# Cluster codes turned in packs of four, two or one tile, two lower halves on GpSimd, and a newly planned order, in a routed attention and MLP kernel

## The chip, the cores and the metric

The kernel runs on one core of a Trainium2 chip. The core has TensorE (PE in the profile; its weight loads are the row PEld), VectorE (DVE), ScalarE (ACT), GpSimd (POOL) and SyncE (SP, which here only issues DMAs), each with its own queue of instructions that it works off in order. The metric is the device time of one execution in microseconds. It was 307.97 us before the change, the median of three runs (307.48 to 308.44).

## The reference

```python
# q, k, v: (4, 8, 768, 64), centroids: (8, 16, 64), w_in: (512, 2048), w_out: (2048, 512)
q_assign = argmax(einsum('bhsd,hcd->bhsc', q_n, c_n))      # q_n, k_n, c_n: divided by their norms
k_assign = argmax(einsum('bhsd,hcd->bhsc', k_n, c_n))
mask = q_assign[:, :, :, None] == k_assign[:, :, None, :]
scores = where(mask, q @ k.T / 8, -1e9)
attn = exp(scores - max) / (sum + 1e-9)
x = (attn @ v).transpose(0, 2, 1, 3).reshape(3072, 512)
h = x @ w_in
out = (h / (1 + exp(-h))) @ w_out
```

A query sees only those keys whose nearest of 16 centroids, by angle, is its own. The kernel does it with a code of 16 numbers per query and key that is 16384 (or a number like it) at the nearest centroid and 0 elsewhere: with the codes as 16 more rows under the 64 of q and k, one matmul of 80 rows gives score and mask together, and the exponential makes the unmasked ones vanish.

## The kernel before

Work comes in four batches of eight heads; a head has six tiles of 128 queries and keys, and heads go in four pairs. Every pair goes through these stages:

- **Loads.** SP loads k, q and v of a pair as natural tiles nk, nq, nv (`load_k`, `load_q`, `load_v`; L374, L389, L404). v is cast to vt (L415, L417).
- **Part** (`part`, from L474). Each element of q and k is split in a high f16 half (L527 on ScalarE, L529 on VectorE, L531 on GpSimd) and a lower half, the rest (L535, VectorE), in a tile hl. The tiles are turned so that the 64 dimensions become partitions, multiplied with the centroids (logits), the best centroid is marked, and the marks are turned too, which gives the code rows.
 - In batches 1 to 3 a DMA turns the tiles (L550, `ab<-hl`); logits are L624, their sums L641, the peak L661, the distance L673 (GpSimd), the marks L700 and L702, and a 32x32 turn on VectorE (L715) gives ohT, from which four copies, one for each 32 columns, place the codes in ab (L732 on GpSimd three times, L728 as a DMA once; `PUTB` names the engines).
 - In batch 0 TensorE turns them: twelve or sixteen tiles of 128x128 (L570), a settle of eight at a time from PSUM to a tile lt (L585, L587), logits L615 and L619, peak L665, marks L690 (written beside the halves in hl, whose rows are 144 wide), and then a second turn of every tile, of its high half and its 16 marks, 80 rows (L570 again), and a settle with a gain for the code rows into ab (L581, L583).
- **Attention** (`attention`). Scores L801 fill a bank of 512 columns, one exponential on ScalarE (L808) makes P of it, PV is L829, and VectorE divides by the sum (L842, L847) into xn. A turn, on TensorE (L877, copies L882, L884) or by DMA (L866), gives xt. Batch 0 goes in two rounds, query tiles 0-1 of all heads and then 2-5, so that the MLP can start early.
- **MLP** (`mlp`). Nine units: batch 0 in three of two tiles, the others in two of three tiles. The 16 up matmul groups (L907), tanh (L913), the gate (L918) into gq, the down matmuls (L942), eviction into ot (L955 ScalarE, L957 VectorE; `EVAC` names one per unit), and the store (L960). `weight` loads the weights on the GpSimd queue (L976, L980), each released by an event of the program that `PW` names.

The order is written by a planner. Every operation is a `step` with an engine, a cost, what it follows, which buffers it holds and a key. `Plan.order` (a list schedule) takes again and again the step that can start first by its costs, the smaller key first among equals, gives it a buffer from a pool and appends it; the instructions are issued in that order, so the costs decide the order on every engine, but not the time. The keys come from `AT` and `ML` (due times of attention rounds and MLP units), `LEADS`, `REST`, `RLOAD` and `SOON` (how far ahead parts and loads go); the pools' sizes stand in `sizes`. Of TensorE's planned waits in the first 80 us (`UNREAD`) the planner fills those that it can with matmuls on zeros (L353), which nobody reads.

Of the kernel before, what the change touches and what calls it, by code (L numbers as in the profile page):

```python
# [11 lines left out]
f16 = mybir.dt.float16  # L12
AF = mybir.ActivationFunctionType
# [20 lines left out]
class Plan:  # L34
# [6 lines left out]
    EARLY = 700  # L41
    TURNED = 1000
    PORT = 0.75

# [4 lines left out]
    def step(self, eng, w, fn, after=(), use=(), key=0.0, load=None, hold=0.0, pace=None, flip=False, lag=None, slack=0.0, port=False):  # L49
# [4 lines left out]
        s.port = port or eng == "POOL"  # L54
# [20 lines left out]
    def order(self):  # L75
# [17 lines left out]
        def complete(s, end):  # L93
# [6 lines left out]
            for x in waits.get(s.n, ()):  # L100
                need[x.n] -= 1
                if not need[x.n]:
                    at = x.hold
                    for a in x.after:
                        late = a.end
                        if a.eng == x.eng and a.load is None:
                            late = a.start + a.w
                        at = max(at, late)
                    engines[x.eng]["ready"].append((at, x))

        def landing(until):

            while True:
# [6 lines left out]
                end = now + first[1] * len(active)  # L120
# [4 lines left out]
                for h in active:  # L125
                    h[1] -= (stop - now) / len(active)
                clock[0] = stop
                if stop == end:
                    s = first[2]
                    rings[s.eng].pop(0)  # L130
                    tail = self.TURNED if s.flip else self.EARLY if s.start < 2000 else self.LAND
# [67 lines left out]
def kernel(  # L199
# [28 lines left out]
    OHV = 16384.0  # L228
    VW = 72
    WN = 32  # L230
    HW = 2 * D + HC
# [6 lines left out]
    def many(name, n, shape, dt):  # L238
# [5 lines left out]
    stk = const.tile([128, H, 3 * HC], f16, name="stk")  # L244
    gain = const.tile([128, 1], f32, name="gain")
# [6 lines left out]
    chl = const.tile([128, 2, D], f16, name="chl")  # L252

    sizes = {
        "nk": (4, [128, 2, NJ * D], f32),
        "nq": (5, [128, 2, NJ * D], f32),
        "nv": (2, [128, 2, NJ * D], f32),
        "hl": (3, [128, 2 * (NJ + NA) * HW], f16),
        "lt": (2, [128, 2 * (NJ + NA), 128], f16),
        "ab": (5, [128, 24, 128], f16),  # L260
        "vt": (10, [128, NJ * VW], f16),
        "P": (18, [128, 512], f16),
        "gq": (7, [128, 4, MOST], f16),
        "xt": (3, [128, NR, S], f16),
        "xn": (3, [128, NJ, 128], f16),
        "L": (2, [128, 2 * NJ, HC], f32),
        "mx": (2, [128, 18], f32),
        "Df": (2, [128, 2 * NJ, HC], f32),
        "oh": (2, [128, 2 * NJ, 32], f16),
        "ohT": (3, [128, 2 * NJ, 32], f16),  # L270
        "tn": (3, [128, MOST], f32),
        "ot": (2, [128, DM], f32),
        "rz": (3, [128, NJ], f32),
    }
    T = {n: many(n, c, shape, dt) for n, (c, shape, dt) in sizes.items()}
    pools = {n: Pool(c) for n, (c, _, _) in sizes.items()}
# [23 lines left out]
    PW = [11, 5, 7, 13, 12, 27, 17, 2, 21, 10, 14, 19]  # L300
    UNREAD = 80000.0
    COLD = 8500.0
    MORE = 250.0
# [4 lines left out]
    VC = ["ACT", "ACT", "POOL", "ACT"]  # L308
    VB = "POOL"
    TK = ["ACT", "ACT", "DVE", "DVE", "DVE"]  # L310
    TQ = ["DVE", "ACT", "DVE", "DVE", "DVE"]
    TR = ["ACT", "DVE", "DVE", "DVE"]
    TS = ["ACT", "DVE", "DVE", "DVE"]
    HI = ["ACT", "ACT", "ACT", "POOL"]
    HR = ["DVE", "POOL", "DVE", "POOL"]
    LEADS = [27.5, 133.1, 88.1]
    REST = [3, 6, 3, 11]
    RLOAD = [2, 0, 3, 0]
    SOON = [7, 4, 7, 4]
    XT = ["DVE", "ACT", "ACT", "DVE"]  # L320
    EVAC = ["DVE", "DVE", "DVE", "DVE", "DVE", "DVE", "DVE", "ACT", "ACT", "DVE"]
# [4 lines left out]
    def consts_v():  # L326
        for t in T["oh"]:
            nc.vector.memset(t, 0.0)
        nc.vector.memset(stk, 0.0)
# [4 lines left out]
    def consts_p():  # L334
        nc.gpsimd.memset(half, 0.5)
        nc.gpsimd.memset(gain[0:64], 1.0)
        nc.gpsimd.memset(gain[64 : 64 + HC], OHV)
# [10 lines left out]
    s_ones = [v_ones(i) for i in range(sizes["vt"][0])]  # L348
# [17 lines left out]
    def load_k(b, p, key, eng="SP", hs=(0, 1), pace=None):  # L366
# [9 lines left out]
        s = step(eng, ISSUE, f, use=[x], key=key, load=657 * len(hs), pace=pace, slack=LATE if b else 0)  # L376
# [4 lines left out]
    def load_q(b, p, key, j0=0, j1=NJ, eng="SP", hs=(0, 1), pace=None):  # L381
# [9 lines left out]
        s = step(eng, ISSUE, f, use=[x], key=key, load=110 * (j1 - j0) * len(hs), pace=pace, slack=LATE if b else 300 if eng == "ACT" else 0)  # L391
# [7 lines left out]
    def load_v(b, p, key, pace=None):  # L399
# [6 lines left out]
        s = step("SP", ISSUE, f, use=[x], key=key, load=1310, pace=pace, slack=LATE if b else 0)  # L406
# [28 lines left out]
    def c_split():  # L435
        nc.vector.tensor_scalar(out=cz, in0=cy, scalar1=1e-6, scalar2=2.0 ** -11, op0=ALU.add, op1=ALU.mult)
        nc.vector.reciprocal(ci, cz)
        nc.vector.tensor_scalar(out=chl[:, 0, :], in0=craw, scalar1=ci, scalar2=None, op0=ALU.mult)
        nc.vector.scalar_tensor_tensor(
            out=chl[:, 1, :], in0=craw, scalar=ci, in1=chl[:, 0, :], op0=ALU.mult, op1=ALU.subtract  # L440
        )
# [3 lines left out]
    def c_turn():  # L445
        nc.tensor.transpose(banks[pc.i].bitcast(f16)[:, 0:128], chl.rearrange("p a d -> p (a d)"), ident)

    def c_place():
        pt = banks[pc.i].bitcast(f16)
        hi = pt[0:64, 0:128].rearrange("d (h c) -> d h c", c=HC)  # L450
        nc.vector.tensor_copy(stk[0:64, :, 0:HC], hi)
        nc.vector.tensor_copy(stk[64:128, :, 0:HC], hi)
        lo = pt[64:128, 0:128].rearrange("d (h c) -> d h c", c=HC)
        nc.vector.tensor_copy(stk[64:128, :, 2 * HC : 3 * HC], lo)

    def c_place_far():
        lo = banks[pc.i].bitcast(f16)[64:128, 0:128].rearrange("d (h c) -> d h c", c=HC)
        nc.vector.tensor_copy(stk[0:64, :, HC : 2 * HC], lo)

    s = step("ACT", 420, load_c, key=-100, load=60, slack=450)  # L460
    s = step("DVE", 400, c_sq, after=[s], key=-50)
    s = step("POOL", 500, c_root, after=[s], key=-90)
    s_split = s = step("DVE", 900, c_split, after=[s], key=-50)
    s = step("PE", 150, c_turn, after=[s, s_ident], use=[pc], key=-50)
    s_cent = step("DVE", 600, c_place, after=[s, s_const], use=[pc], key=-50)
    s_far = step("DVE", 200, c_place_far, after=[s, s_const], use=[pc], key=0)


# [5 lines left out]
    def part(b, p, segs, a0, due, lead=20.0, hi_eng="POOL", turn="DMA", twin=False, sub="POOL", code_eng=None, pace=None, wait=None):  # L474
# [10 lines left out]

        pitch, HI_AT = (2 * D, 0) if turn == "DMA" else (HW, D)

        def tiles_of(hl):
            return T["hl"][hl.i][:, 0 : n * pitch].rearrange("p (n c) -> p n c", c=pitch)

        t0 = 0
        runs = []
        for kind, h, j0, j1 in segs:
            runs.append((kind, h, j0, j1, t0))
            t0 += j1 - j0
        merged = []
        for r in runs:
# [595 lines left out]
```

## Time and profile before

| | |
|---|---|
| median of three runs | 307.97 us |
| profiled execution | 307.14 us, span of the instructions 305.3 us |
| busy: PE, DVE, ACT, POOL | 297.3, 207.9, 223.7, 108.2 us |
| first scores, first tanh, first batch logits | 11.8, 36.0, 51.6 us |
| DMA | 41.82 MB, mean 137 GB/s |
| granted TensorE clock | 0.998 |

The span is the time from the first to the last instruction of the program; the profiled execution's own time is 1.8 us longer. A group in the profile is one line of the kernel on one engine with what it writes and reads, its count, its busy time in us and the mean ns of one; behind the second bar stands how long the engine was idle before them and what ended that. In the chain and in timelines the first two numbers are start and length in us. A busy TensorE is not TensorE at its peak, since matmuls overlap; their distance from start to start says more.

### The profile page before, as it was taken

The page shows a single profiled execution, that of the slowest core. Times are in us where ns is not written, and L with a number is a line of the kernel's source. Part 1 is how long each engine was busy: PE and PEld are TensorE (multiplying, and loading weights), DVE is VectorE, ACT ScalarE, POOL GpSimd, SP SyncE. Part 2 cuts the span into 40 slices and gives each one's busy share as a digit, 9 for nine tenths or more (in the row PEclk, how much of TensorE's full clock was granted, in tenths as well). Part 3 has the DMA queues.
Part 4 walks back from the last instruction along what each step waited for, and adds up shares of the span by engine and source line. Part 5 has one row for each costly group of instructions (what it writes and reads, how often), then busy time and mean ns, then how long its engine had stood idle before and what let it go on. Part 6 is the DMA issues. An engine that isn't in the chain of part 4 may idle for free.

```text
span 305.3 us, 8425 instructions
## 1 busy us (share of the span) xinstructions
PE 297.3 (97%) x3257; PEld 196.1 (64%) x3257; DVE 207.9 (68%) x493; ACT 223.7 (73%) x461; POOL 108.2 (35%) x218
## 2 busy tenths in 40 slices
PE   8999999999999999999999998999999999999995
PEld 6898777577677746666656765665655565554644
DVE  5999688778869955989766997867562323750820
ACT  5869999888988838999777998778782380642721
POOL 2546432656466480717564563733000000000000
PEclk9999999999999999999999999999999999999999
DMA  7999969993969888486969848472010201002001
GB/s 245 290 249 251 206 104 224 103 248 87 226 100 237 191 167 196 138 156 162 237 149 223 155 154 169 131 129 66 0 37 36 84 12 71 35 0 73 32 34 69
DMA packets 73688, 41.82 MB, mean 137 GB/s; under 512 B 53041, under 2 KB 70705, under 8 KB 73649
## 3 DMA queue, kind: packets, MB, share of 16 engines
q1 hardware_dynamic: 68944, 36.94, 51.4%
q0 software_dynamic: 4288, 4.20, 8.6%
q8 instruction: 25, 0.41, 0.6%
q10 hardware_dynamic: 416, 0.16, 0.2%
q14 instruction: 15, 0.11, 0.1%
HBM read 27.30 MB, written 6.29 MB: 110 GB/s over the span
## 4 chain that ended last, share of the span: by engine, by line
PE 80%; DMA 7%; ACT 5%; DVE 3%; issue 1%; POOL 1%; SPq 0%; ACTq 0%; POOLq 0%
PE bank L942 27%; PE bank L907 22%; PE bank L801 16%; PE bank L829 9%; ACT P L808 4%; DMA ab<-hl 3%; PE bank L570 3%; DMA wout_s<-in_moe_w_out_dram 2%; PE bank L624 2%; DMA nk<-in_k_dram 2%; POOL hl L531 1%; PE bank L615 1%; DVE hl L535 1%; DVE gq L918 1%; PE bank L619 1%
## 5 line engine op out<-in xcount | busy, mean ns | idle before, releaser
L808 ACT ACTIVATE P<-bank 128x512 f16<-128x512 f32 x288 | 157.8, 640 | 30.8 <-PE bank L801 29.1
L942 PE MATMUL bank<-wout_s,gq 128*128 128x512 f16 (+1 forms) x400 | 97.1, 370 | 0.4 <-DMA wout_s<-in_moe_w_out_dram 0.4
L907 PE MATMUL bank<-xt,win_s 128*128 128x384 f16 (+1 forms) x576 | 95.6, 308 | 0.0
L918 DVE SCALAR_TENSOR_TENSOR gq<-tn,bank 128x384 f16<-128x384 f32 (+1 forms) x144 | 70.1, 504 | 32.4 <-ACT tn L913 28.7
L801 PE MATMUL bank<-ab 80*128 80x256 f16 (+1 forms) x384 | 90.9, 326 | 0.0
L913 ACT ACTIVATE tn<-bank 128x384 f32<-128x384 f32 (+1 forms) x144 | 67.8, 488 | 24.1 <-PE bank L907 20.9
L907 PEld LDWEIGHTS <-win_s 128*128 128x128 f16 x576 | 55.0, 97 | 28.8
L942 PEld LDWEIGHTS <-gq 128*128 128x128 f16 x400 | 37.9, 98 | 33.1 <-issue 0.7
L829 PEld LDWEIGHTS <-P 128*128 128x128 f16 x1152 | 45.6, 97 | 11.9 <-ACT P L808 0.8
L829 PE MATMUL bank<-vt,P 128*128 128x65 f16 x1152 | 49.8, 193 | 0.7 <-ACT P L808 0.6
L732 POOL COPY ab<-ohT 16x384 f16<-16x384 f16 x72 | 39.3, 546 | 28.2 <-DVE ohT L715 11.7
L801 PEld LDWEIGHTS <-ab 80*128 80x128 f16 x384 | 34.6, 97 | 20.7 <-DVE ab L583 0.2
L673 POOL TENSOR_TENSOR Df<-L,mx 128x192 f32<-128x192 f32 x24 | 12.3, 511 | 41.9 <-DVE mx L661 39.7
L957 DVE COPY ot<-bank 128x512 f32<-128x512 f32 x18 | 12.3, 681 | 16.4 <-PE bank L942 15.6
L535 DVE SCALAR_TENSOR_TENSOR hl<-nk,hl 128x384 f16<-128x384 f32 (+1 forms) x29 | 19.8, 687 | 3.3 <-POOL hl L531 3.1
L535 DVE SCALAR_TENSOR_TENSOR hl<-nq,hl 128x384 f16<-128x384 f32 (+3 forms) x33 | 20.9, 635 | 0.6 <-POOL hl L531 0.3
L641 DVE TENSOR_REDUCE L<-bank 128x192 f32<-128x384 f32 x24 | 13.3, 552 | 10.0 <-PE bank L624 9.7
L847 DVE TENSOR_TENSOR xn<-bank,rz 128x384 f16<-128x384 f32 (+2 forms) x40 | 19.1, 477 | 1.4 <-DVE rz L842 0.2
L531 POOL TENSOR_SCALAR hl<-nk 128x384 f16<-128x384 f32 (+1 forms) x25 | 13.6, 547 | 7.6 <-PE bank L570 6.7
L955 ACT COPY ot<-bank 128x512 f32<-128x512 f32 (+1 forms) x7 | 3.7, 524 | 17.2 <-PE bank L942 17.2
L531 POOL TENSOR_SCALAR hl<-nq 128x384 f16<-128x384 f32 (+2 forms) x27 | 15.2, 566 | 1.7 <-DMA nq<-in_q_dram 1.1
L417 POOL CAST vt<-nv 128x384 f16<-128x384 f32 x26 | 14.6, 582 | 1.1 <-DMA nv<-in_v_dram 0.7
(60 smaller groups left out, 183.6 us busy)
## 6 DMA issues: line engine op xcount, KB each, us to landing
nv<-in_v_dram SPq DMA_DIRECT2D x16, 384.0 KB, 5.6
out_dram<-ot SPq DMA_DIRECT2D x23, 256.0 KB, 2.3
nk<-in_k_dram SPq DMA_DIRECT2D x15, 384.0 KB, 4.3
nq<-in_q_dram SPq DMA_DIRECT2D x12, 384.0 KB, 4.7
wout_s<-in_moe_w_out_dram POOLq DMA_DIRECT2D x8, 256.0 KB, 7.2
win_s<-in_moe_w_in_dram POOLq DMA_DIRECT2D x4, 512.0 KB, 9.3
nq<-in_q_dram SPq DMA_DIRECT2D x4, 256.0 KB, 6.5
nk<-in_k_dram SPq DMA_DIRECT2D x2, 192.0 KB, 2.8
```

Of the source, the lines that this page charges most:

```text
L417: (nc.gpsimd if eng == "POOL" else nc.vector).tensor_copy(dst, src)
L531: nc.gpsimd.tensor_scalar(out=dh, in0=src, scalar1=qs, scalar2=1.0, op0=ALU.mult, op1=ALU.mult)
L535: nc.vector.scalar_tensor_tensor(out=dl, in0=src, scalar=qs, in1=dh, op0=ALU.mult, op1=ALU.subtract)
L732: nc.gpsimd.tensor_copy(dst, src)
L801: nc.tensor.matmul(banks[sb.i][:, at : at + 128 * (c1 - c0)], ab[0:80, kt[j], :], ab[0:80, qt + c0 : qt + c1, :].rearrange("p n c -> p (n ...
L808: nc.scalar.activation(out=T["P"][P.i][:, 0:at], in_=banks[sb.i][:, 0:at], func=AF.Exp, bias=0.0, scale=ESC if b else -ESC)
L829: nc.tensor.matmul(banks[O.i][:, (D + 1) * t : (D + 1) * t + nn], w, vt[:, VW * j : VW * j + nn], start=(j == 0), stop=(j == NJ - 1), skip ...
L847: nc.vector.tensor_tensor(out=T["xn"][xn.i][:, 0:nq, (h % 2) * D : (h % 2) * D + D], in0=banks[O.i][:, 0 : (D + 1) * nq].rearrange("p (t c ...
L907: nc.tensor.matmul(banks[bank.i][:, 0:n], win_s[:, r, ts(fb, 128)], T["xt"][xtb[b].i][:, r, 128 * j0 : 128 * j1], start=(r == 0), stop=(r ...
L913: nc.scalar.activation(out=T["tn"][tn.i][:, 0:n], in_=banks[bank.i][:, 0:n], func=AF.Tanh, bias=0.0, scale=1.0)
L918: nc.vector.scalar_tensor_tensor(out=T["gq"][g.i][:, fb % 4, 0:n], in0=T["tn"][tn.i][:, 0:n], scalar=1.0, in1=banks[bank.i][:, 0:n], op0=A ...
L942: nc.tensor.matmul(banks[bank.i][:, 0 : c1 - c0], T["gq"][gqs[fc // 4].i][:, fc % 4, ts(t, 128)], wout_s[:, fc, c0:c1], start=(fc == 0), s ...
```

## The change

- **Codes in packs (batch 0).** The marks no longer stand in hl but in a tile oh, 32 columns per tile of the sequence. Four tiles of marks are turned by TensorE at once (128 columns, L734 of the new kernel; for some pairs two or one, the letters "2" and "1"), which leaves the codes of tile g at partitions 32g to 32g+15. `put_near` and `put_alone` bring them to rows 64 to 79 of ab, each by the engine that its letter in `TQ` or `TS` names: D and A straight from PSUM with a factor, P by GpSimd from a copy oc that VectorE makes of PSUM. The first settle writes ab itself (lt and the gain are gone), so the high halves aren't turned twice.
- **Centroids.** High and low part of the centroids are turned in two turns and placed by one copy.
- **Lower halves on GpSimd.** Where `LO` has a P (one part, of two heads) GpSimd does both halves in three passes over a tile xs (`both`).
- **Attention and MLP.** PV sums of the two heads of a pair share a bank where there are two query tiles, with one reciprocal and one product; up groups of 256 columns go in pairs, with one tanh and one gate of 512.
- **Puts of batches 1 to 3.** `PUTB` is two copies on VectorE and two on GpSimd in place of three on GpSimd and a DMA.
- **The planner.** Its costs (DMA tails and rates, the cost of a dependent step on VectorE, shares of the DMA rings) and all its parameters are new: due times, leads, engines, the count of buffers in each pool (`COUNT`), the events that release the weights. Pools that shrink: nk 4 to 2, nq 5 to 3, nv 2 to 1, ab 5 to 3, vt 10 to 4, gq 7 to 4, xt 3 to 1. The order is a new one on all engines: the first up matmul stands behind 63 units of scores (35 before), fillers number 74 (42 before), all in the first 45 us.

```diff
-    EARLY = 700
+    EARLY = 280
...
+    SHARE = 1.19
+    OWN = 110.0
...
-                            late = a.start + a.w
+                            late = a.start + a.w + (self.OWN if a.eng == "DVE" else 0.0)
...
+    COUNT = [2, 3, 1, 4, 3, 4, 17, 4, 1, 12, 1, 6, 11, 11, 18, 4, 4, 34, 4, 3]
...
-    PW = [11, 5, 7, 13, 12, 27, 17, 2, 21, 10, 14, 19]
-    UNREAD = 80000.0
+    PW = [3, 6, 8, 13, 18, 28, 15, 4, 3, 13, 20, 37]
+    UNREAD = 45000.0
...
-    LATE = 600
-    AT = [32.0, 63.0, 104.0, 133.9, 193.2, 273.6]
-    ML = [55.5, 127.6, 75.5, 138.3, 182.4, 254.3, 222.5, 316.0, 335.3, 350.3]
-    PUTB = ["POOL", "POOL", "SP", "POOL"]
+    LATE = 1000
+    AT = [-1051.0, -65.0, 93.6, 199.4, 269.1, 441.6, 569.0, 825.3, 934.9, 1275.5, 1380.2]
+    ML = [-325.7, 429.6, 82.9, 595.5, 964.7, 479.3, 1406.6, 860.8, 1553.0, 1722.9]
+    PUTB = ["DVE", "DVE", "POOL", "POOL"]
...
-    TQ = ["DVE", "ACT", "DVE", "DVE", "DVE"]
-    TS = ["ACT", "DVE", "DVE", "DVE"]
+    TQ = ["DDDP", "DDPP", "DDDD", "2DA", "2DD"]
+    TS = ["DDDD", "1DA", "PPPP", "DDPP"]
+    LO = ["D", "P", "D", "D"]
...
+            def both(views=views, qs=qs, m=m):
+                src, dh, dl = views()
+                x = T["xs"][xs.i][:, 0 : 64 * m].rearrange("p (h j d) -> p h j d", h=src.shape[1], d=D)
+                nc.gpsimd.tensor_scalar(out=x, in0=src, scalar1=qs, scalar2=1.0, op0=ALU.mult, op1=ALU.mult)
+                nc.gpsimd.tensor_copy(dh, x)
+                nc.gpsimd.tensor_tensor(out=dl, in0=x, in1=dh, op=ALU.subtract)
...
-            for c in chunks:
-                bank = buf("M")
-                x = step("PE", 57 * len(c), turn_of(c, bank, D, HW), after=[marks, his, s_ident], use=[hl, bank], key=key + 12 * span)
...
+                def turn_code(c0=c0, c1=c1, bk=bk):
+                    for i in range(c0, c1, side):
+                        m = min(side, c1 - i)
+                        at = (i - c0) // side * 128
+                        nc.tensor.transpose(
+                            banks[bk.i].bitcast(f16)[0 : 32 * m, at : at + 128],
+                            T["oh"][oh.i][:, i : i + m, :].rearrange("p n c -> p (n c)"), ident,
+                        )
...
+                def settle_code():
+                    nc.vector.tensor_copy(T["oc"][oc.i][:, 0:wide], banks[bank.i].bitcast(i16)[:, 0:wide])
...
+                    def put_alone(c0=c0, c1=c1, bk=bk, on_a=on_a, cols=cols, g=g):
+                        dst = T["ab"][A.i][64 : 64 + HC, a0 + c0 + g : a0 + c1 : side, :]
+                        src = banks[bk.i].bitcast(f16)[32 * g : 32 * g + HC, 0:cols].rearrange("p (n c) -> p n c", c=128)
...
+                def put_near(g=g, cols=cols):
+                    dst = T["ab"][A.i][64 : 64 + HC, a0 + g : a0 + n : 4, :]
+                    rows = slice(32 * g, 32 * g + HC)
+                    if near[g] in "PS":
+                        src = T["oc"][oc.i][rows, 0:cols].rearrange("p (n c) -> p n c", c=128)
+                        if near[g] == "P":
+                            nc.gpsimd.tensor_copy(dst, src)
...
+        both = 2 if 2 * nq * (D + 1) <= 512 else 1
...
+        m = 512 // n if n >= 128 and NFB % (512 // n) == 0 and 512 // n <= 2 else 1
+        for fb in range(0, NFB, m):
```

More of the change, by code (lines that the diff above doesn't have):

```diff
@@ L119, in landing @@
                 first = min(active, key=lambda h: h[1])
[L120 removed]
+                parts = len(active) ** self.SHARE
+                end = now + first[1] * parts
                 later = [h[0] for h in heads if h[0] > now]
@@ L472, with part @@
     score_uses = {}
-    def part(b, p, segs, a0, due, lead=20.0, hi_eng="POOL", turn="DMA", twin=False, sub="POOL", code_eng=None, pace=None, wait=None):
+    def part(b, p, segs, a0, due, lead=20.0, hi_eng="POOL", turn="DMA", twin=False, sub="POOL", code_eng=None, pace=None, wait=None, lo_eng="D"):
         key = due - lead
```

472 lines of the change are left out of this document (246 added, 226 removed).

## The prediction

> **What bounds the kernel now.** I read the busy table first, then the chain that ended last, the groups by form, the waits, and the engines' timelines for the first 48 us. TensorE is busy from end to end, and the chain is TensorE for 80% of the span:
>
> ```profile
> PE 297.3 (97%) x3257; PEld 196.1 (64%) x3257; DVE 207.9 (68%) x493; ACT 223.7 (73%) x461; POOL 108.2 (35%) x218
> PE 80%; DMA 7%; ACT 5%; DVE 3%; issue 1%; POOL 1%; SPq 0%; ACTq 0%; POOLq 0%
> ```
>
> Busy is not useful: modelled ends overlap and 42 matmuls are fillers on zeros. So I count matmuls by form and multiply by their distance start to start in TensorE's timeline (0.216 us for 512 columns, 0.162 for 384, 0.109 for 256, 0.056 for a turn of 128, 0.029 for a PV matmul, 0.025 for logits). The chain's pieces show the same distances, 32 turns in 1.79 us and 48 down matmuls in 10.36:
>
> ```profile
> 13.31 1.79 PE bank L570 x32
> ...
> 270.49 10.36 PE bank L942 x48
> 280.85 10.40 PE bank L907 x64
> 291.25 10.41 PE bank L942 x64
> ```
>
> Down 83.0, up 83.1, scores 62.8, PV 33.4, turns (96+96+30) 12.4, logits (480) 12.0: 286.7 us of work. The last matmul starts at 301.4, so 4.6 us of fillers and 10.1 us of nothing are all there is to win besides the work; 3.9 us follow it (eviction and store). Where the nothing lies: 25.3 us of work stand before the first up matmul, which starts at 34.9, so fillers and waits cost 9.6 by then; after it 5.1 are lost, of which 2.9 in six waits (0.55 for the output weights, 2.1 in four waits of the batch logits L624 for their turned tiles, 0.22 in a PV) and 2.2 as a few ns per matmul. The first part is set by ScalarE and VectorE, which are almost full there while TensorE waits for them; later only TensorE is full (columns: stretch, its length, then busy time and count of PE, PEld, DVE, ACT, POOL):
>
> ```profile
> 12.00:36.00 24.00, 23.25 (x424) 20.37 (x423) 21.66 (x60) 21.21 (x44) 12.09 (x23) 1.00 1.11 245
> 36.00:60.00 24.00, 23.55 (x327) 16.76 (x325) 19.22 (x50) 22.44 (x53) 10.89 (x22) 1.00 0.93 154
> 60.00:210.00 150.00, 148.55 (x1734) 98.68 (x1733) 118.67 (x282) 127.05 (x264) 81.11 (x152) 1.00 0.77 167
> ```
>
> and, of the waits, the one that the logits of batches 1 to 3 have (total, times, longest):
>
> ```profile
> PEld L624 <- DMA ab<-hl: 3.5, 6, 1.2
> ```
>
> The groups that the change touches:
>
> ```profile
> L583 DVE TENSOR_SCALAR ab<-bank,gain 80x1024 f16<-80x1024 f16 x10 | 7.3, 741 | 1.2 <-PE bank L570 0.9 <-ACT P L808 0.3
> L570 PE MATMUL bank<-ident,hl 128*80 128x128 f16 x96 | 6.9, 219 | 0.0
> L732 POOL COPY ab<-ohT 16x384 f16<-16x384 f16 x72 | 39.3, 546 | 28.2 <-DVE ohT L715 11.7 <-PE bank L801 6.8 <-PE bank L907 2.8
> L587 DVE COPY lt<-bank 128x1024 f16<-128x1024 f16 x9 | 5.9, 684 | 0.2 <-PE bank L570 0.2
> L585 ACT COPY lt<-bank 128x1024 f16<-128x1024 f16 x3 | 3.0, 1015 | 0.0
> ```
>
> **TensorE's work.** The 96 second turns (80 rows, one per tile) become 38 (14 of four tiles, 16 of two, 8 of one), the turns of the attention result 30 become 16, the centroids' one becomes two. 71 turns less at 0.056: **-4.0 us**, on the path, since TensorE is the bound. Everything else on TensorE keeps its count, so the work is 282.7. Fillers go from 42 to 74 (8.1 us); they stand where the planner expects a wait, so I count them with the waits.
>
> **The stage before the first up matmul.** The new order puts 32.4 us of work before it (25.3 now), because 60 exponentials instead of 33 stand before ScalarE's first tanh. That ScalarE queue, by start-to-start times: 60 x 0.48 = 28.8, seven settles of 1024 columns x 0.89 = 6.2 (three now, plus two gain settles of 1.0), four v casts x 0.41 = 1.6, high parts 2.9, one x copy 0.25, table load 1.3: 41.0 us, against 28.2 now. ScalarE idles 7.0 us before its first tanh now (at 35.96): 4.5 before the first exponential, 2.5 behind it, of which 2.2 for a v load whose casts now go to GpSimd. So the first tanh comes between 41.0+4.5 = 45.5 and 41.0+7.0 = 48.0; I take 47.0, nearer the middle, because VectorE is nearly as full and feeds it in small pieces. The first up group (8 x 0.109 and 0.2 of delay) starts 1.1 before: 45.9. Fillers and waits by then: 45.9 - 32.4 = 13.5, where now they are 9.6 (they are still 9.6 when 32.4 of work is done, at 42.0). **+3.9 us.** The saved turns are thus eaten by an attention stage that runs at ScalarE's pace: an exponential takes ScalarE 0.48, and its scores and PV take TensorE 0.33 (0.216 + 4 x 0.029).
>
> What else lies there is beside it. VectorE: ten code settles (0.66 apart) become four copies (0.2), five puts of 1024 columns (0.64), four of 512 (0.38) and eleven of 256 (0.24), 8.1 for 6.6, and five tile settles instead of nine (-2.4); merged norms and recips -1.0; eleven memsets of the code tiles at 0.26 instead of two at 0.21 hold the first centroid square from 3.6 to 4.0, and the first logits, now at 8.2, stay within 0.5 because the first turns no longer stand behind the centroids' turn. Its 36.3 us before the first gate end before ScalarE's 41.0 (pair 1's k lands at 6.3 and its high part takes 1.15 on GpSimd, so from 7.6 on VectorE has 30.3 us queued: 38 without a hole, 9 before the first up group). GpSimd: nine puts of 256 columns, 0.36 to 0.54 each by L732; the lower split of one pair is three passes of 512 elements there (0.57 and 0.45-0.6 by L531 and L417, the subtraction 1.3 by L673's 0.48 for 192), 2.4 in place of 0.6; behind it wait four weight loads and four puts. VectorE's settle of that pair waits for it, and with it VectorE's queue; by the sum VectorE is there at 18.5, GpSimd ends its passes about then or 1 us behind. Those 9 us of VectorE's cover it: 0, other end +1. Evictions move partly to ScalarE (11 x 0.6), which idles at the end. Up pairs make one tanh of 512 (0.48) of two of 256 (0.28), 24 times, and gates 0.60 of 2 x 0.33: -1.9 on ScalarE, -1.4 on VectorE, hidden under up pairs of 0.87.
>
> **The later stages.** Batches 1 to 3 lose 24 small DMAs and 24 GpSimd puts; VectorE gets 48 puts of 16x384. No row has that: between L702's 0.20 for 96 elements and L715's 0.58 for 384; I take 0.33, from the 0.415 of L884's 512. That is 16 us more on VectorE, less some 5 for gates and evictions, where it is 118.67 of 150 busy: room, so 0. On SP the waits behind the small DMAs go (23.3 us in 15 waits for L715 alone); off the path. Only one xt buffer is left: all four turns of a batch go out on SP after the last up matmul of the batch before. Three issues of 1.24 and a landing of 2.5 to 5.3 are 6.2 to 9.0, and the order leaves 9.2 to 9.8 us of TensorE work between: 0, with +1.5 at each of three places as the other end if SP is late. Fewer nk, nq, nv and vt buffers tie loads to casts, and casts to PVs; the planner's allowance for landings grows from 0.6 to 1.0, so the logits stand 0.4 later behind their turned tiles. Of the waits of 0.16, 0.29, 0.54 and 1.10 that takes 1.25; the weights' 0.55 goes too, since the first down matmul moves from 52 to 53 while its three pieces are released by exponentials 20, 26 and 46. **-1.8 us**; ends -2.9 and +3.
>
> **Sum** on the profiled execution: 307.14 (span 305.3 and 1.8 around it) - 4.0 + 3.9 - 1.8 = 305.2; the median of the runs shown is 0.8 above that execution, so **306.1**.
>
> [...] VectorE's and GpSimd's timelines show oh<-Df taking 0.51 beside a GpSimd instruction; the fastest takes 0.20:
>
> ```profile
> 124.73 0.51 DVE L702 TENSOR_SCALAR oh<-Df 128x96 f16<-128x96 f32 x1 [0.23 <-POOL Df L673]
> 124.67 0.98 POOL L531 TENSOR_SCALAR hl<-nk 128x384 f16<-128x384 f32 x2
> ```
> If each part's second VectorE put so waits for one GpSimd put of 0.54, VectorE gets 24 x 0.54 = 13 us more. [...]
>
> **Rivals.** (1) The plan holds: ScalarE is never short after its first exponential, the first tanh comes at 45.5, and all six later waits go: -1.5 and -1.1 more, 303.5. For it: ScalarE is full from 25 to 50 now. Against: its 33 exponentials had 2.5 of holes. [...] (3) Nothing gained: first tanh at 48.0 and the later waits as now, +1.0 and +1.8: 308.9, within 0.3% or just over.
>
> **Numbers.** Forecast (305 to 307) 0.42, rival 1 0.14, rival 3 0.20, rival 2 with the xt turns late 0.24. Range 303.5 to 310, from rival 1 to rival 2; the likeliest case's own is 304.8 to 307.2. What a measurement can tell is 0.3%, 0.9 us: faster 0.56, same 0.16, slower 0.28 (rival 2 and a fifth of rival 3).
>
> **What would show it.** Right: 3144 real matmuls (71 less) and 74 fillers; the first tanh at 46 to 48 with ScalarE over 95% busy from 26 on; the first up matmul near 46; the batch logits waiting under 1 us in all; code puts on VectorE near 0.33. Wrong: a first tanh before 45 or behind 49, a TensorE wait over 1 us behind xt<-xn or an ab put of VectorE, or puts above 0.7 us.

## The result: 0.8% slower

Six runs of the changed kernel have a median of 309.87 us (309.63 to 310.73), six of the kernel before beside them 307.38 (306.31 to 308.44): a ratio of 1.0083, 95% interval 1.0059 to 1.0107. The profiled execution took 310.04 us with a span of 308.3, against 307.14 and 305.3. The forecast was 306.1, faster; the time lies inside the range, the sign is wrong.

The profile after: the busy table and the engines' shares of the chain that ended last.

```profile
PE 299.6 (97%) x3218; PEld 195.8 (64%) x3218; DVE 218.2 (71%) x517; ACT 221.4 (72%) x440; POOL 101.4 (33%) x201
...
PE 79%; DVE 7%; ACT 6%; DMA 5%; issue 1%; POOL 0%; DVEq 0%; ACTq 0%; POOLq 0%
```

TensorE has 39 instructions less and is busy 2.3 us more: what was saved in turns came back as fillers and as a longer span. The stretches (length, then busy time and count of PE, PEld, DVE, ACT, POOL, then the granted clock, the DMA share, GB/s):

```profile
12.00:36.00 24.00, 23.61 (x419) 19.34 (x418) 17.82 (x46) 21.16 (x42) 16.49 (x31) 1.00 1.14 245
36.00:60.00 24.00, 23.63 (x284) 16.57 (x281) 18.82 (x50) 21.45 (x45) 8.67 (x19) 1.00 0.80 146
60.00:210.00 150.00, 147.77 (x1608) 95.82 (x1607) 121.52 (x281) 114.76 (x230) 59.23 (x112) 1.00 0.66 157
```

VectorE is less busy from 12 to 36 than before (17.82 against 21.66), GpSimd more (16.49 against 12.09), ScalarE the same: the stage is not bound by the sum of VectorE's work. Its end, in ScalarE's timeline (start, length):

```profile
36.64 13.51 ACT L855 ACTIVATE P<-bank 128x512 f16<-128x512 f32 x27
49.72 0.92 ACT L972 ACTIVATE tn<-bank 128x512 f32<-128x512 f32 x1
```

Twenty-seven exponentials without a hole, and only then the first tanh, at 49.7 (35.96 before). The groups that carry the new code path, from the groups by form:

```profile
L710 POOL COPY ab<-ohT 16x384 f16<-16x384 f16 x48 | 25.4, 530 | 33.0 <-issue 17.7 <-DVE ohT L694 4.1 <-PE bank L848 3.1
...
L712 DVE COPY ab<-ohT 16x384 f16<-16x384 f16 x48 | 20.0, 417 | 1.2
...
L766 DVE TENSOR_SCALAR ab<-bank 16x1024 f16<-16x1024 f16 x5 | 3.4, 684 | 2.2 <-PE bank L734 2.1
...
L791 DVE TENSOR_SCALAR ab<-bank 16x256 f16<-16x256 f16 x11 | 3.1, 286 | 0.2
```

and TensorE's waits behind transposing DMAs (logits of batches 1 to 3) and behind the gates (down projection): in all, times, longest.

```profile
PEld L613 <- DMA ab<-hl: 2.5, 3, 1.4
...
PE bank L613 <- DMA ab<-hl: 1.5, 3, 1.0
PEld L1000 <- DVE gq L977: 1.2, 3, 0.6
...
PE bank L1000 <- DVE gq L977: 0.9, 2, 0.5
```

Counted as in the prediction (matmuls of a form times their start-to-start distance; the rest of the time up to a matmul's start is "fillers and waits"):

| kernel | real work | first up starts | fillers and waits by then | after it |
|---|---|---|---|---|
| before | 286.7 | 34.9 | 9.7 | 5.0 |
| changed | 282.7 | 48.4 | 16.0 | 5.5 |

So -4.0 + 6.3 + 0.5 = 2.8 of the 2.9 us between the two profiled executions. At 15 us of real work done, 13.2 us are lost already (9.2 before); the rest is lost on the way to the first up.

The order itself says why the first tanh is so late. The MLP needs the first round (round 0) of all eight heads, six score matmuls of 256 columns for each head. In the kernel before, all 48 of them go first. In the changed kernel 36 go first, from 12.1 us, then 20 of 512 columns, which are of the second round (round 1), from 27.0, and the 12 of the last two heads only from 37.7. The theories under test:

- **A**: the smaller buffer counts (k loads 4 to 2, q loads 5 to 3, v loads 2 to 1, ab 5 to 3, v tiles 10 to 4) let the last heads of round 0 start only when others have been through round 1. By A the packs have no part in it.
- **B**: the packs' chain (marks, turn, copy, puts) delays the early stage in any order.
- Several smaller ones: buffers cost at run time (C), fillers (D, E), the new puts on VectorE as the cause of the later waits (H), the choice of settings (F, G).

### The profile page after: what moved, and what is told of

The parts are those of the page before. It is cut to its first block, busy times and chain, and to the rows that moved or that the text cites. A ratio compares the mean times of both kernels' runs of the same rounds, so it can differ in the third digit from the quotient of the medians.

```text
span 308.3 us, 8200 instructions
## 1 busy us (share of the span) xinstructions
PE 299.6 (97%) x3218; PEld 195.8 (64%) x3218; DVE 218.2 (71%) x517; ACT 221.4 (72%) x440; POOL 101.4 (33%) x201
## 4 chain that ended last, share of the span: by engine, by line
PE 79%; DVE 7%; ACT 6%; DMA 5%; issue 1%; POOL 0%; DVEq 0%; ACTq 0%; POOLq 0%
PE bank L1000 25%; PE bank L966 24%; PE bank L848 14%; PE bank L879 8%; DMA ab<-hl 5%; ACT P L855 4%; PE bank L360 3%; PE bank L613 2%; PE bank L577 1%; DVE gq L977 1%; ACT ab L586 1%; DVE hl L548 1%; ACT tn L972 1%; DVE ab L712 1%; PE bank L734 1%
## 5 line engine op out<-in xcount | busy, mean ns | idle before, releaser
L855 ACT ACTIVATE P<-bank 128x512 f16<-128x512 f32 x288 | 154.2, 659 | 24.1 <-PE bank L848 23.4
L1000 PE MATMUL bank<-wout_s,gq 128*128 128x512 f16 (+1 forms) x400 | 95.4, 370 | 0.9 <-DVE gq L977 0.9
L966 PE MATMUL bank<-xt,win_s 128*128 128x384 f16 (+1 forms) x576 | 89.7, 308 | 0.0
L848 PE MATMUL bank<-ab 80*128 80x256 f16 (+1 forms) x384 | 89.1, 325 | 0.5 <-ACT P L855 0.2
L972 ACT ACTIVATE tn<-bank 128x384 f32<-128x384 f32 (+1 forms) x120 | 64.1, 558 | 35.1 <-PE bank L966 27.8
L977 DVE SCALAR_TENSOR_TENSOR gq<-tn,bank 128x384 f16<-128x384 f32 (+1 forms) x120 | 67.0, 575 | 31.3 <-ACT tn L972 27.1
L879 PEld LDWEIGHTS <-P 128*128 128x128 f16 x1152 | 45.5, 97 | 10.4 <-issue 0.7
L710 POOL COPY ab<-ohT 16x384 f16<-16x384 f16 x48 | 25.4, 530 | 33.0 <-issue 17.7
L1015 DVE COPY ot<-bank 128x512 f32<-128x512 f32 (+1 forms) x14 | 9.1, 652 | 18.5 <-PE bank L1000 18.4
L630 DVE TENSOR_REDUCE L<-bank 128x192 f32<-128x384 f32 x24 | 13.3, 554 | 10.9 <-PE bank L613 7.3
L712 DVE COPY ab<-ohT 16x384 f16<-16x384 f16 x48 | 20.0, 417 | 1.2
L905 DVE TENSOR_TENSOR xn<-bank,rz 128x384 f16<-128x384 f32 (+1 forms) x36 | 18.3, 509 | 0.9
L537 POOL TENSOR_SCALAR hl<-nq 128x384 f16<-128x384 f32 (+2 forms) x27 | 14.8, 549 | 0.5 <-DMA nq<-in_q_dram 0.2
```

The lines of the kernel that those rows point to most:

```text
L537: nc.gpsimd.tensor_scalar(out=dh, in0=src, scalar1=qs, scalar2=1.0, op0=ALU.mult, op1=ALU.mult)
L710: nc.gpsimd.tensor_copy(dst, src)
L712: nc.vector.tensor_copy(dst, src)
L848: nc.tensor.matmul(banks[sb.i][:, at : at + 128 * (c1 - c0)], ab[0:80, kt[j], :], ab[0:80, qt + c0 : qt + c1, :].rearrange("p n c -> p (n ...
L855: nc.scalar.activation(out=T["P"][P.i][:, 0:at], in_=banks[sb.i][:, 0:at], func=AF.Exp, bias=0.0, scale=ESC if b else -ESC)
L879: nc.tensor.matmul(banks[O.i][:, at : at + D + 1], T["P"][P.i][:, col : col + 128], vt[:, VW * j : VW * j + D + 1], start=(j == 0), stop=( ...
```

## The experiments

### Buffer counts: three kernels

More buffers for q and v loads, ab and v tiles in the changed kernel, planned anew by its own planner. The k loads stay at two; pools that stood half empty are cut to make room, and no other setting is touched:

```diff
-    COUNT = [2, 3, 1, 4, 3, 4, 17, 4, 1, 12, 1, 6, 11, 11, 18, 4, 4, 34, 4, 3]
+    COUNT = [2, 5, 2, 4, 5, 10, 17, 4, 1, 6, 1, 6, 4, 7, 4, 4, 4, 34, 4, 3]
```

> The changed kernel with five buffer counts as large as before the change (q loads 3 to 5, v loads 1 to 2, operand buffers ab 3 to 5, v tiles 4 to 10; other pools that stand half empty are cut so that it fits), and planned anew by its own planner: nothing else is edited. The order that comes out has 35 exponentials ahead of the first tanh instead of 60. Theory A (the early stage starves because the last heads of round 0 wait for buffers that round 1 of other heads must free first): the first up matmul moves from 48.4 to 36-39 us, fillers and waits by then from 16.0 to 11.5-13 us. With the later waits left at 5.5 us the time is 306-307.5; the remaining settings were not chosen for these counts, so later waits may take back up to 4 us (to 310). Theory B (the packs' own chain of marks, turn, copy and puts makes the early stage late in any order): fillers and waits at the first 15 us of real TensorE work stay at 13 us and are 15-16 us at the first up, the time 309.5-311.

Measured: 312.96 us, ratio 1.0166 (1.0111 to 1.0222). The first up moved to 36.6, and fillers and waits by then fell from 16.0 to 12.8. All 48 score matmuls of round 0 go ahead of round 1 again, and ScalarE's timeline has the first tanh at 38.05:

```profile
31.35 6.96 ACT L855 ACTIVATE P<-bank 128x512 f16<-128x512 f32 x14 [0.39 <-PE bank L848]
38.05 1.94 ACT L972 ACTIVATE tn<-bank 128x512 f32<-128x512 f32 x3
```

A's early part holds, with 3.2 us. The total doesn't: 11.1 us are lost after the first up (5.5 in the changed kernel), in waits for gates, for transposing DMAs and in many small ones of the scores. I put this down to the remaining settings, which were chosen for another order; with settings chosen for larger counts the later runs lose 6.5 to 7.2 there. The time was above both theories' ranges.

The reverse, the kernel before with fewer load buffers and no packs:

```diff
-        "nk": (4, [128, 2, NJ * D], f32),
-        "nq": (5, [128, 2, NJ * D], f32),
-        "nv": (2, [128, 2, NJ * D], f32),
+        "nk": (2, [128, 2, NJ * D], f32),
+        "nq": (3, [128, 2, NJ * D], f32),
+        "nv": (1, [128, 2, NJ * D], f32),
```

> The kernel before with only the load buffers of the changed one (k loads 4 to 2, q loads 5 to 3, v loads 2 to 1), planned anew by its own planner; no packs, no other edit. Its order has 45 exponentials ahead of the first tanh instead of 33. Theory A (buffer counts make the early stage late): first tanh from 36.0 to 43-46 us, fillers and waits by the first up matmul from 9.6 to 14-16 us, time 311.5-314 (4 to 6 us more than before). Theory B (the packs make it late): without packs the fillers and waits stay at 10-11.5 us by the first up and the time is 307.5-309.

Measured: 320.11 us, ratio 1.0348 (1.0257 to 1.0439); first up at 51.3 behind the 45 exponentials, fillers and waits by then 22.3. The order takes A's form without any packs (36 score matmuls of round 0, 12 of round 1, then the last 12 of round 0), and the loss is larger than A's range. Its two largest waits for loads, and two stretches of it:

```profile
POOL hl L531 <- DMA nk<-in_k_dram: 7.1, 1, 7.1
...
POOL hl L531 <- DMA nq<-in_q_dram: 6.2, 1, 6.2
```

```profile
31.00:35.00 4.00, 1.39 (x20) 1.22 (x18) 1.39 (x3) 1.94 (x3) 0.40 (x1) 0.92 1.17 254
35.00:38.00 3.00, 3.00 (x27) 1.35 (x25) 0.89 (x2) 2.43 (x6) 0.96 (x2) 0.50 1.15 268
```

Late loads leave TensorE idle for 2.8 us, and then the clock is granted at 0.50 until 44.6, which A had not counted. The one run of four with a mean clock of 1.00 took 315.99, still above A's 311.5 to 314. How much of this is the order and how much the lateness of the loads by itself, the run doesn't separate.

The changed kernel's order kept, its buffers dealt out of larger pools:

> The changed kernel with every instruction in the same order on its engine, its buffers dealt round larger pools (k loads 4, q loads 5, v loads 2, ab 5, v tiles 10, gate tiles 6, xt 2, and smaller ones where pools stand half empty), with six small GpSimd memsets more. Theory A (buffers act through the order that they force on the planner): the order stands, so first up stays at 47.5-48.7 us, and the time within 1 us of the changed kernel's 310 (309-310.5). Theory C (the waits for buffers at run time, such as GpSimd's 18 waits of 56 us in all for a v tile, cost by themselves): first up 2 to 4 us earlier or the 5.5 us of later waits cut by half, time 306-308.

```diff
-    T = {n: many(n, c, shape, dt) for c, (n, (shape, dt)) in zip(COUNT, sizes.items())}
+    MADE = [4, 5, 2, 4, 5, 10, 17, 6, 2, 6, 1, 6, 4, 4, 3, 4, 2, 4, 3, 1]
+    T = {n: many(n, c, shape, dt) for c, (n, (shape, dt)) in zip(MADE, sizes.items())}
...
+            free = min(x for x in out_of[n])
...
+            out_of[n].remove(free)
+            out_of[n].append((ends[id(b)], free[1]))
+            b.i = free[1]
```

Measured: 310.53 us, ratio 1.0081 (1.0056 to 1.0107), first up at 49.2 (0.5 later than expected), 16.8 us by then, 6.2 after. C falls: GpSimd's 56 us of waits for v tiles in the changed kernel are gone here, and no time is won. So in the changed kernel the counts act through the order that they force on the planner, not through waits at run time. (This kernel also has 4 memsets of code tiles at the start instead of 11, and gains nothing by it.)

### Fillers and puts

Without the 40 filler matmuls behind 9 us:

```diff
     for s in plan.order():
+        if s.key == 1e9 and s.start > 9000:
+            continue
         s.fn()
```

> The changed kernel without the 40 filler matmuls (0.109 us each, 4.4 us in all) that stand after 9 us; all else in the same order. Theory A and B alike (they fill time in which TensorE waits for its data anyway): first up within 0.5 us of 48.4, the same time within 0.6 us (309.3-310.6), with the 4.4 us turned into waits. Theory D (the 32 fillers more than before hold real matmuls up): first up 1 to 3 us earlier, time 307-309. Theory E (without them the granted clock falls): TensorE's clock below 1.0 between 9 and 48 us and the time over 311.

Measured: 309.03 us, ratio 1.0034 (1.0005 to 1.0063); first up at 48.5 and 16.1 us by then, unchanged. So the added fillers are not what holds the early stage up. Theory E is right in part about the clock (where in the run it fell isn't recorded), though not about the time: seven of the ten runs have a mean clock of 0.987 to 0.994, where the six of the changed kernel have 0.999 or more. The time came out below the range by 0.3. The profiled execution was the fastest of the ten (308.25, clock 1.00), so it can explain the median only in part: it has 3.7 us instead of 5.5 after the first up, where waits of 1.1, 0.45 and 0.43 for ab<-hl don't occur. Three of these DMAs between 95 and 110 took 3.7 to 4.9 us to land here, 4.8 to 5.4 in the changed kernel, though it issued the first and the last of them 0.25 us earlier. As I read it, this order leaves the logits no slack for that spread.

With the fillers gone the profile shows what TensorE waits for up to the first up (matmuls, then weight loads):

```profile
PE bank L848 <- DVE ab L791: 0.9, 1, 0.9
PE bank L848 <- ACT P L855: 0.8, 1, 0.8
PE bank L879 <- ACT P L855: 0.8, 3, 0.3
```

```profile
PEld L734 <- DVE oh L671: 1.3, 5, 0.3
...
PEld L848 <- DVE ab L791: 1.0, 1, 1.0
```

It is spread: marks (L671) ahead of the code turns, code puts (L791, and 0.3 for L766) ahead of the scores, exponentials ahead of PV and of scores. Of the matmuls' own waits 1.4 us are behind marks and puts and 1.6 behind exponentials. No single wait exceeds 1.1.

The puts of batches 1 to 3 on the engines of before:

```diff
+                    where = ["POOL", "POOL", "SP", "POOL"][g]
-                    if code_eng[g] == "SP":
+                    if where == "SP":
```

> The changed kernel in the same order, the 96 code puts of batches 1 to 3 run on the engines of before (72 on GpSimd, 24 as DMA issues of SyncE, none on VectorE). [...] Theory A (the later waits are on DMA transposes and gates that stand too close in this order): 5-6.5 us stay, time 309.5-311; GpSimd, 0.39 us a put, may add up to 1 us of its own.

Measured: 319.78 to 329.03 us in four runs, far above the 309.5 to 311 of theory A. Three of the four lie near 329 at a mean clock of 0.963 to 0.967, the fastest had 0.989; the profile is of one of the three (328.55). In it TensorE waits behind the very puts that were moved:

```profile
PE bank L847 <- DMA ab<-ohT: 6.3, 4, 2.6
PE bank L847 <- POOL ab L709: 4.2, 2, 3.5
```

Part of the excess is the granted clock behind such waits, 0.50 in the second of these stretches:

```profile
64.00:71.00 7.00, 3.76 (x49) 2.11 (x47) 2.17 (x7) 3.03 (x6) 2.01 (x4) 0.87 0.83 215
71.00:76.00 5.00, 5.00 (x31) 2.68 (x28) 3.08 (x8) 3.14 (x7) 2.91 (x6) 0.50 0.12 39
```

H isn't borne out: in this order the engines of before are much worse, by 9.9 us even in the fastest run. What VectorE's 48 puts cost by themselves this run can't tell, since it brings waits of its own; the changed kernel's profile lists no TensorE wait behind one of them.

### The settings

Larger counts as in the first experiment, with priorities, due times, engines and pack forms chosen anew for them by the end that the planner itself gives:

> The changed kernel's code with the larger buffer counts of the first experiment (q loads 5, v loads 2, ab 5, v tiles 10) and priorities, due times, engine choices and pack forms of its planner chosen anew for these counts; all 48 turns of codes of batch 0 still go in packs. 41 exponentials stand ahead of the first tanh. Theory A (the packs do save TensorE work and cost little by themselves; what was lost lay in the order that the small counts force): real work 282-283 us, fillers and waits 10-12 us by the first up matmul (36-39 us) and 2 to 5 us after it, time 303.5-306.5, faster than before. Theory B (the packs' chain of marks, turn, copy and puts delays the early stage in any order): fillers and waits 13 us or more at the first 15 us of real work, time 307.5 or more.

Measured: 308.18 us, ratio 0.9996 (0.9961 to 1.0031). First up at 40.0, 14.2 us by then (11.4 at the first 10 us of real work, 11.7 at 15), 6.8 after. Neither theory as stated: the packs' kernel is no slower than before and so misses A's range, the time lies in B's range, but B's 13 us at the first 15 of real work don't occur. By the first up 2 us more are lost than A allowed, and at the first 10 us of real work it is 3.2 more than in the kernel before (8.2).

The same for the kernel before, and for the changed kernel with its own small counts (only settings differ in both, so no diff):

> The kernel before with its priorities, due times and engine choices chosen anew in the same way as in the run beside it, its code and buffer counts untouched: what such a new choice gives without packs. Theory A: the order of before is already near its best, fillers and waits by the first up matmul stay at 9.5-10.5 us of 286.7 us of real work, time 306.5-309. Rival F (it is the new choice of settings that gains, not the packs): as much faster than before as the run beside it, 303.5-306.

Measured: 318.04 us, ratio 1.0304 (1.0232 to 1.0376); 12.7 us by the first up, 14.3 after it. F falls: a new choice by the planner's costs is no gain in itself, and can be a large loss. It also means that any one run with settings chosen anew is a single draw.

> The changed kernel with its own small buffer counts and its settings chosen anew in the same way. 59 exponentials still stand ahead of the first tanh. Theory A (small counts force the late first up, whatever the settings): first up at 46-48.5 us, fillers and waits by then 14-16 us, time 308-311. Rival G (it was only an unlucky choice of settings): first up before 42 us, time below 306.5.

Measured: 307.32 us, ratio 1.0000 (0.9968 to 1.0031); first up at 46.4, 14.8 us by then, 4.5 after, work 282.0. The small counts do keep the first up late (A), yet the whole loss of the change in time, 2.6 us, goes with other settings: in the profiled executions 1.2 early, 1.0 later, 0.7 in x turns given to DMA. Neither theory has the time: it lies below A's 308 to 311 and above G's 306.5. The first up is A's.

### The packs alone, and true step times

All code tiles of batch 0 turned singly in the changed kernel:

```diff
-    TQ = ["DDDP", "DDPP", "DDDD", "2DA", "2DD"]
-    TS = ["DDDD", "1DA", "PPPP", "DDPP"]
+    TQ = ['1D', '1D', '1D', '1D', '1D']
+    TS = ['1D', '1D', '1D', '1D']
```

> The changed kernel with its packs undone and nothing else: every code tile of batch 0 is turned alone, and its code rows are put from PSUM by VectorE, 12 puts in place of 29 puts and 4 copies; planned anew by its own planner with the same settings and counts, 60 exponentials ahead of the first tanh as before. Theory B' (the packs' finer chain of marks, turn, copy and puts costs about 2 us of the early stage by itself, beside what the buffer counts cost): real work 285.5-286.5 us, fillers and waits at 10 us of real work from 11.5 to 9-10.5 us, by the first up from 16.1 to 13-14.5 us, time 309.5-311.5. Theory A alone (only the counts cost): fillers and waits stay at 15.5-16.5 us by the first up, time 312.5-314.

Measured: 309.73 us, ratio 1.0055 (1.0021 to 1.0088), with 3.3 us more of real work (286.0): with these settings the packs were worth nothing. Fillers and waits at 10 us of real work were 10.0 (11.5 with packs), as B' has it. What follows in the trace can't be used: the profiled execution took 313.06, 3.3 above the median. In it a q load landed late at 20 us (GpSimd waited 2.5 us for it), and behind that the granted clock was 0.54 in the mean of 23 to 26.

```profile
20.70:23.00 2.30, 0.61 (x16) 0.49 (x12) 0.16 (x2) 1.07 (x3) 2.15 (x4) 1.00 1.16 262
23.00:26.00 3.00, 3.00 (x46) 2.64 (x43) 2.57 (x4) 0.81 (x2) 0.51 (x1) 0.54 1.17 250
```

Then I compared the planner's step times with the trace of the changed kernel. It counts 0.7 us for the 11 memsets at the start, which take 3.05. It counts 0.47 for a low part of 384 columns on VectorE, which takes 0.62 to 0.65 in the mean, and the centroids' steps are 0.06 to 0.25 short each. For high parts on GpSimd the trace shows little of the 0.09 that is added (0.51 to 0.53 against 0.49 counted). With these changed, 1.2 us more allowance for each transposing DMA, the larger counts and settings chosen anew for all this (a part of the edit):

```diff
-    s_const = step("DVE", 700, consts_v, key=-100)
+    s_const = step("DVE", 250 + 275 * len(T["oh"]), consts_v, key=-100)
...
-            los.append(step("DVE", dve_w(64 * m, 1.05), lo, port=True, after=[x, lds, wait], use=[nat, hl], key=key + span))
+            los.append(step("DVE", dve_w(64 * m, 1.05) + 80, lo, port=True, after=[x, lds, wait], use=[nat, hl], key=key + span))
...
-            turned = [step("SP", 120 * n, turn_dma, after=[his, los], use=[hl, A], key=key + 2 * span, load=195 * n, flip=True, slack=LATE)]
+            turned = [step("SP", 120 * n, turn_dma, after=[his, los], use=[hl, A], key=key + 2 * span, load=195 * n, flip=True, slack=LATE + 1200)]
```

> Packs with the larger buffer counts again, now with step times in the planner that the traces of the changed kernel show (the start's 11 memsets 3.05 us where it counts 0.7; low parts on VectorE, high parts on GpSimd and the centroids' steps 0.06 to 0.15 us longer each) and 1.2 us more allowance for every transposing DMA; settings chosen anew for these. 32 exponentials stand ahead of the first tanh. Theory A with B' (both early losses come from an order that the counts and the planner's too short step times made): real work 282.5-283.5 us, fillers and waits 9.5-11.5 us by the first up matmul (33-36 us) and 2.5-4.5 us after it, time 302-305, faster than before. Rival I (the packs bring waits that no order takes away): fillers and waits 13 us or more by the first up, or 6 us or more after it, time 307 or more.

Measured: 305.28 us (304.35 to 306.10, 11 runs), ratio 0.9910 (0.9880 to 0.9939), faster than both kernels. Real work 283.5 (14 turns more than the changed kernel: some of the first codes are turned singly, later ones in packs), first up at 34.7, 10.9 us by then, 6.5 after. Its busy table:

```profile
PE 296.3 (97%) x3201; PEld 194.1 (64%) x3201; DVE 205.3 (67%) x476; ACT 222.7 (73%) x440; POOL 118.1 (39%) x233
```

Rival I falls on the early stage and on the time. Its other sign, 6 us or more after the first up, did come: the later waits are over the 2.5 to 4.5 expected, and the time is 0.3 above the range.

> As the run beside it, with a second choice of settings found from another start (34 exponentials ahead of the first tanh, 33 puts of code rows where the other has 22): a check that the result is not that of one lucky order. Theory A with B': fillers and waits 10-12 us by the first up, 2.5-5 us after it, time 302.5-305.5. Rival I: 307 or more.

Measured: 306.78 us, ratio 0.9966 (0.9934 to 0.9997); 12.6 us by the first up (35.7), 7.2 after. Both counts are over what was expected, and the time 1.3 above its range; a second order confirms the sign, with a third of the gain. Two draws of settings for the same code lie 1.5 us apart.

> The code, counts, corrected step times and allowance of the fastest run so far, with every pack of one tile (12 puts straight from PSUM, no copies) and settings chosen anew for that: what the packs are worth when both have an order made for them. 34 exponentials stand ahead of the first tanh. Real work 286-286.5 us (3.2 more than with packs). Theory K (with an early stage that is not held up, the packs keep most of their gain): fillers and waits 10-11 us by the first up and 5-7 after it as there, time 306.8-308.8, 1.5 to 3.5 us slower than with packs. Rival J (their finer chain costs what the turns save, in any order): fillers and waits lower by 2 us or more, time 304.5-306.

Measured: 307.40 us, ratio 1.0007 (0.9983 to 1.0031): no faster than before, 2.1 us slower than the first order with packs and 0.6 slower than the second. Real work 285.3 (below the 286 to 286.5 expected, since the new settings give more x turns to DMA), 12.2 us by the first up, 5.4 after. K has the time right, and J's 304.5 to 306 did not come. The first order with packs saves 1.8 us of real work against this one, 40 code turns fewer at 0.056 less some x turns, and keeps about that much in time. With 1.5 us between two draws of settings this shows the direction, not the size.

## Why the prediction was wrong

**TensorE's work, -4.0.** Right: 286.7 to 282.7 in the trace, 71 turns and no other count changed; fillers 74, 8.1 us.

**The stage before the first up, +3.9.** This step failed; it measured +6.3. Of its form much was right: 60 exponentials ahead of the first tanh, ScalarE setting the end. But "I take 47.0" was 49.7, outside its own 45.5 to 48.0 and behind the 49 that it names as a sign of being wrong. Two terms were too small.

The first is the ScalarE queue: 42.2 us for the 41.0 of the sum. The price of 0.48 for an exponential holds in the solid run (36.64 to 49.72 for 27, 0.484 each), but all 60 took 29.3 for 28.8, the settles 6.6 for 6.2, the high parts 3.1 for 2.9, the casts 1.7 for 1.6. A check was at hand: the same prices gave 28.2 for the queue before, which with its 7.0 us of idle time ends at 35.2 and not at 35.96.

The second is ScalarE's idle time, taken as 6.0, between today's two values; it was 7.5. Of that 5.1 lie before the first exponential (4.5 in the kernel before). These are its waits up to the first tanh; the other 0.7 is the start:

```profile
ACT P L855 <- PE bank L848: 2.8, 3, 1.3
ACT ab L586 <- PE bank L577: 2.2, 2, 1.7
ACT hl L533 <- DMA nk<-in_k_dram: 1.7, 2, 1.2
```

So ScalarE waited for TensorE's scores and turns, and part of what TensorE waited for in turn is the marks and puts that the run without fillers shows one by one. VectorE's many small code instructions I had put under "What else lies there is beside it". VectorE did have room (17.8 of 24 us busy), but each tile goes through mark, turn, copy and put, and TensorE waits for the last: a chain's latency and not a sum of busy time. How much of the 1.5 us of idle time over the estimate is this chain isn't shown. The nearest figure is the run without packs, 1.5 us less lost at 10 us of real work.

**What lay behind it.** The smaller counts were priced only for the later stages ("Fewer nk, nq, nv and vt buffers tie loads to casts"). Their real effect was to force the order of round 0 and round 1. I had read the order off, not its cause, so this explains why the kernel is late in its early stage rather than why the sum for that order was too small. The first two experiments show it both ways, in size 3.2 us for the counts in the changed kernel. Counts, settings and step times together bring it to 5.1 of the 6.3 in the fastest kernel. What the step times alone do isn't shown, since they were changed together with the allowance and the settings.

**The later stages, -1.8.** This step failed by as much: +0.5, 2.3 over the forecast where the early stage is 2.4 over. Either miss alone uses up the 1.9 us of gain that was forecast. The batch logits were to wait "under 1 us in all"; counted from start to start, three waits took 2.0 (1.13, 0.45, 0.43), and two behind gates 1.2. I took a larger allowance in the planner to mean more slack behind each DMA; these waits show that there was none at these places. What sets the loss after the first up, 3.7 to 7.2 us with packs apart from the first experiment's 11.1, and 5.0, 5.4 and 14.3 in three of the orders without, I haven't isolated. The profiles of the changed kernel and of the run without late fillers suggest that part of it is how long the transposing DMAs take to land: 4.8 to 5.4 us for three of them in the one, 3.7 to 4.9 in the other.

**Costed at nothing.** The single xt buffer: right, no up matmul waited for xt<-xn. The 48 puts: 0.417 in the mean against 0.33 taken, under the 0.7 that the prediction names as a sign of being wrong, VectorE 121.5 of 150 busy, and the profile lists no TensorE wait behind them. That holds for this order: in the fastest kernel TensorE waited 0.7 us for one such put. Rival 2, with 310 the upper end of the range, took 13 us more on VectorE, 24 puts that each wait for a GpSimd put of 0.54. No run shows this term: it was my estimate from one instruction that took 0.51 us beside a GpSimd one and 0.20 at its fastest. What the trace shows in its place is 48 puts of 0.25 to 0.58 us, 4.2 us more in all than taken. So rival 2 named the time for waits that didn't occur: that was luck. The triple on GpSimd took 2.4, as estimated.

**The rivals.** Nothing gained (308.9) was nearest in mechanism: first tanh late, later waits as before. Its first tanh of 48.0 was still too early by 1.7. That the time lies inside the range owes something to the same luck, since rival 2 set the upper end.

## To carry to other kernels

Saved work on the bound engine is only a gain if the stage ahead isn't made later by as much: 4.0 us saved here met 6.3 lost. Before trusting prices for a new order, let them reproduce the old one; here they missed it by 0.7 us. Where one instruction is split into a chain, look also at the time until its last consumer may start, which busy shares don't show. Where a planner orders the work, a smaller pool is a change of order; ask which late task a buffer is held for. A planner's step times are worth comparing with the trace before its order is believed: a start of 3.05 us counted as 0.7 stood in this one. The kernel with such corrections, more allowance and new settings is 0.9% faster than before and a second one 0.3%, but which of these made the gain isn't separated.

## Unexpected on the hardware

The granted clock fell to half after single holes in TensorE's work, and cost about as much as the hole or more. It was 0.50 for 10.2 us behind a wait of 2.8 (34.4 to 44.6 us, the kernel before with fewer buffers), for 3.4 us behind one of 1.85 (23.2 to 26.7, codes turned singly in the changed kernel) and for 3.4 us behind one of 1.05 (22.0 to 25.4, the last experiment). At half rate 3.4 us of work lose 1.7, and 10.2 lose 5.1. But waits of 2.17 and 1.98 in the kernel before with new settings, and one of 1.3 in the fastest kernel, left it at 1.00.

The length of the hole alone doesn't decide it, since one of 1.05 us was enough and one of 2.17 was not. What decides, these runs don't show.

The profiled execution of the changed kernel stayed at 1.00 until its last matmul. Without the late fillers the profiled one did too, but seven of ten runs have a mean of 0.987 to 0.994. By an estimate from these figures, a mean of 0.994 over 308 us is what one stretch of 3.4 us at half rate gives, so the fillers seem to have kept such stretches away. The time was no worse without them (309.03 against 309.87).
